# Attention, experts and second layer on one core: clears planned behind the scatters, one PSUM set, small DMAs moved off GpSimd's queue

## The chip, the cores and the metric

One core of a Trainium2 chip runs the whole program. The time is that of one execution on the device, in microseconds (us); the kernel before takes 758.77 us (median of 3 runs, 758.49 to 759.9). The engines are TensorE (PE; PEld is its weight load), VectorE (DVE), ScalarE (ACT), GpSimd (POOL) and SyncE (SP), which mainly issues DMAs.

## The reference, cut to what matters

Three layers follow each other: a linear attention with a decayed state, a top-1 mixture of 8 experts, and a dense two-matrix layer.

```python
for t in range(S):                                  # batch 4, heads 8, S 768, head_dim 48
    state = alpha[:, :, t, :, None] * state + np.einsum('bhd,bhe->bhde', k[:, :, t], v[:, :, t])
    y[:, :, t] = np.einsum('bhd,bhde->bhe', q[:, :, t], state)
x = y.transpose(0, 2, 1, 3).reshape(B * S, H * D)   # 3072 tokens of 384
expert_idx = np.argmax(normalised(x) @ normalised(expert_emb).T / tau, axis=1)
for e in range(8):
    mask = expert_idx == e
    h = np.maximum(x[mask] @ w1[e], 0.0)            # 384 -> 1024
    out[mask] = gate_w[mask, None] * (h @ w2[e])    # 1024 -> 384
h = out @ w_in                                      # 384 -> 2048
result = np.maximum(0.01 * h, h) @ w_out            # 2048 -> 384
```

## The kernel before, in words

**First stage, 0 to some 178 us.** Attention runs in 16 units (a batch and two heads each); its last matmuls of a unit are the values (L426, `py<-am,v`), whose sums ScalarE and VectorE copy to `yT` (L469, L471), and TensorE turns these back (L486) for the routing of a batch. The routed rows are written by 6 indirect DMAs of GpSimd for each batch (L609, 24 in all) to `bucket` in DRAM, where each expert owns a region; a row carries 384 values, its scale, its gate and its token's number. `early_rows` (L613 ff.) reads the first 256 rows of expert 0 back as soon as the third batch's scatters have landed, so that expert 0 can begin before the last batch is there. After the last batch VectorE works out at which place of the packed order each expert begins (`offi`, L760).

**Experts, some 178 to 391 us.** Each of 8 experts takes up to CAP = 432 rows. `gather` loads them from `bucket` (`xg`, L921, L924), `block` casts them to two f16 halves `xs` (L976), SP's DMA transposes turn them (`xt<-xs`, L978). `up` (L1036 to L1038) multiplies by w1 into 4 PSUM banks `ps1`; ScalarE and VectorE empty a bank together (`held<-ps`, L1043 and L1044). `down` (L1062 to L1064) multiplies by w2 into 4 banks `ps2`, emptied into the packed `x2h` and `x2l` (L1073, L1074) at a place that each engine loads from `offi` (L1050). Expert 0 goes in two parts, 256 early columns and the other 176. The weights come as pieces through four staging tiles: a DMA on SP (L987), then `w1h<-wstage` on ScalarE (L992) and `w1l<-wstage,w1h` on VectorE (L993). `clear` (L1083) fills the rest of `x2` by 12 ScalarE copies of 128x660. `put_meta` (L935 to L947) copies gate and token number of each expert's rows into the packed `meta` in DRAM: one DMA for expert 0 and two for each of the others, 15 in all, on GpSimd's queue. The chunks of 432 rows overlap (a later expert's rows overwrite the end of the chunk before), so each of these DMAs waits for the one before to have landed.

**Second layer, 391 to 752 us.** 12 groups of 256 columns run through `u` (5 banks, L823 to L825) and `c` (3 banks, L857 to L859); their PSUM pool is opened when that of the experts has been released. `ms` is loaded from `meta` (L1286) and its second column cast to the indices `tki` (L1299), which the output's indirect stores (L891) use.

**What sets the order.** Nothing is scheduled by hardware or compiler here. `Plan` (L31 ff.) takes each step with an engine, a cost, what it reads and writes and a wished time `at`, sets the steps out against each other as if each took its cost, and writes each engine's instructions in the order of the starts that come out of that. Engines then run strictly in this order, and wait by semaphores. A step of `clear` has no reads, so the planner may put it anywhere:

```python
plan.add(S_, 0.16 + w / 1200, lambda x=x: nc.scalar.activation(x, row0[:, 0:1].to_broadcast([P, w]), AF.Copy), [], [("clear", n, d)], at=at)
```

The steps of experts and second layer go through two separate plans, each in a `with tc.manual_schedule():` of its own.

Of the kernel before, what the change touches and what calls it, by code (L numbers as in the profile page):

```python
# [21 lines left out]
P = 128  # L22
# [3 lines left out]
D = H * HD  # L26
# [149 lines left out]
def body(ctx, tc, qT, kT, aT, v, emb, tau, w1, w2, w_in, w_out, out):  # L176
# [24 lines left out]
    nc.gpsimd.dma_start(tau_sb, tau.to_broadcast([P, 1]))  # L201
# [10 lines left out]
    hid = [[held[:, i, f] for f in range(NF1)] for i in range(2)]  # L212
    shared = keep.tile([P, 2 * W64], F32, name="shared")
# [67 lines left out]
    with tc.tile_pool(name="at", bufs=1) as rt, \  # L281
# [53 lines left out]
        nc.gpsimd.dma_start(emb_sb, emb)  # L335
# [83 lines left out]
        def values(i, h):  # L419
            b, hp = divmod(i, NP)  # L420

            def go():
                for n in range(HC):
                    for j in range(2):
                        c, e0 = HC * h + n, (2 * hp + j) * HD
                        nc.tensor.matmul(y_of(c, j), tv[b % 2][:, c, e0:e0 + HD], tam[h][:, j, n], start=c == 0, stop=c == NC - 1)  # L426

# [466 lines left out]
    first = [stage() for _ in range(4)]  # L894
    with tc.tile_pool(name="mx", bufs=1) as mxp, \
            tc.tile_pool(name="w64", bufs=1) as w64, \
            tc.tile_pool(name="wst2", bufs=1) as wst2, \
            tc.tile_pool(name="pm", bufs=1, space=PSUM) as pm:
# [7 lines left out]
        ps1 = [pm.tile([P, CAP], F32, name=f"ps1{i}") for i in range(4)]  # L906
        ps2 = [pm.tile([P, CAP], F32, name=f"ps2{i}") for i in range(4)]
# [27 lines left out]
        def put_meta(e):  # L935
            xg = xgs[e % 2]

            def go():
                if e == 0:
                    nc.gpsimd.dma_start(meta[:CAP], bucket[:CAP, D + 1:D + 3])  # L940
                    return
                so = nc.gpsimd.value_load(offi[0:1, e:e + 1], min_val=0, max_val=NT)
                nc.gpsimd.dma_start(meta[ds(so, NF * P)].rearrange("(n p) c -> p n c", p=P), xg[:, :NF, D + 1:D + 3])
                if CAP % P:
                    nc.gpsimd.dma_start(meta[ds(so + NF * P, CAP % P)], xg[:CAP % P, NF, D + 1:D + 3])

            plan.add(G_, 6.0, go, [("xg", e % 2)] if e else ["bucket"], [("meta", e)], at=begin(e) + 4)  # L947
# [137 lines left out]
        with tc.manual_schedule():  # L1085
            plan.add("WAIT", 10.8, lambda: None, [], ["bucket"])
# [304 lines left out]
```

## Time and profile before

| what | value |
|---|---|
| median of the runs | 758.77 us (758.49 to 759.9) |
| the profiled execution, its own time | 762.96 us |
| span of its trace | 761.3 us |
| mean granted clock of TensorE | 0.99 |
| PE busy | 729.9 us, 96% of the span, 6774 matmuls |
| DVE, ACT, POOL busy | 601.3, 388.4 and 99.8 us |
| DMA | 84.70 MB in 58769 packets, mean 111 GB/s |

TensorE is busy almost always, so the table says little. What a change can win or lose lies in the few stretches where TensorE stands, and the views that show these are the waits, the timeline by engine and the table by stretch. The profiled execution is 4.2 us slower than the median; differences are counted against its own time.

### The profile page before, as it was taken

What the parts mean: (1) busy time and instruction counts of PE and PEld (TensorE: products, weight loads), DVE (VectorE), ACT (ScalarE), POOL (GpSimd) and SP (SyncE); (2) the same over time, 40 slices, a digit from 0 to 9 for tenths busy, and PEclk for the clock granted to TensorE, in tenths of its full rate; (3) what the DMA queues carried; (4) which work ended last, traced back from release to release, by engine and by line L of the source; (5) the groups of instructions that cost most, each with busy time, mean ns of one, the idle gap of its engine ahead of it and who ended that gap; (6) DMA issues with size and microseconds to landing.
All of it is one profiled execution on the core that took longest, in us unless ns stands there. A gap on an engine that the chain in (4) does not pass through costs nothing.

```text
span 761.3 us, 16644 instructions
## 1 busy us (share of the span) xinstructions
PE 729.9 (96%) x6774; PEld 561.6 (74%) x6774; DVE 601.3 (79%) x1131; ACT 388.4 (51%) x746; POOL 99.8 (13%) x108
## 2 busy tenths in 40 slices
PE   7999999967999999999989999999999999999995
PEld 4777767745855555555558777999999999999994
DVE  8989899953887789888869888878768778778761
ACT  3344544535876668767736454544544444445430
POOL 6121715132000100000000011010010110110111
PEclk9999999998999999999999999999999999999998
DMA  8983946233999897886500000000000000000000
GB/s 287 357 284 128 284 147 197 75 112 112 235 244 258 174 239 203 228 231 205 171 1 2 12 11 11 13 22 2 22 22 2 22 22 1 22 22 2 22 23 24
DMA packets 58769, 84.70 MB, mean 111 GB/s; under 512 B 26680, under 2 KB 37952, under 8 KB 58688
## 3 DMA queue, kind: packets, MB, share of 16 engines
q1 hardware_dynamic: 55072, 74.06, 35.2%
q0 software_dynamic: 3616, 9.53, 3.4%
q8 instruction: 55, 0.90, 0.5%
q14 instruction: 26, 0.21, 0.1%
HBM read 66.80 MB, written 12.12 MB: 104 GB/s over the span
## 4 chain that ended last, share of the span: by engine, by line
PE 84%; DVE 7%; DMA 3%; ACT 2%; issue 1%; POOL 1%; another core or an unknown queue 1%; SPq 0%; ACTq 0%; POOLq 0%; DVEq 0%
PE u L823 8%; PE u L824 8%; PE u L825 8%; PE c L857 6%; PE c L859 6%; PE c L858 6%; PE ps L1036 4%; PE ps L1037 4%; PE ps L1038 4%; PE ps L1063 4%; PE ps L1064 4%; PE ps L1062 4%; PE psc L407 3%; DMA v<-in_v 2%; PE py L426 2%; PE py L458 2%
## 5 line engine op out<-in xcount | busy, mean ns | idle before, releaser
L823 PE MATMUL u<-x2h,wih 128*128 128x256 f16 x576 | 157.0, 273 | 2.1 <-DVE x2l L1074 2.1
L824 PE MATMUL u<-x2l,wih 128*128 128x256 f16 x576 | 157.0, 273 | 0.0
L825 PE MATMUL u<-x2h,wil 128*128 128x256 f16 x576 | 157.0, 273 | 0.0
L831 DVE TENSOR_TENSOR held<-u,held 128x512 f32<-128x512 f32 x96 | 65.9, 687 | 56.0 <-ACT held L830 55.9
L830 ACT ACTIVATE held<-u 128x512 f32<-128x512 f32 x96 | 57.3, 597 | 86.5 <-PE u L825 83.1
L891 POOL DMA_INDIRECT out<-wstage,tki x24 | 25.2, 1049 | 437.0 <-DVE wstage L870 257.1
L1063 PE MATMUL ps<-held,w2h 128*128 128x432 f16 (+2 forms) x216 | 70.2, 326 | 0.3 <-DVE held L1044 0.3
L1062 PE MATMUL ps<-held,w2h 128*128 128x432 f16 (+2 forms) x216 | 70.2, 326 | 0.0
L1064 PE MATMUL ps<-held,w2l 128*128 128x432 f16 (+2 forms) x216 | 70.2, 326 | 0.0
L1037 PE MATMUL ps<-xt,w1h 128*128 128x432 f16 (+1 forms) x192 | 63.6, 333 | 0.8 <-DVE xt L962 0.8
L1036 PE MATMUL ps<-xt,w1h 128*128 128x432 f16 (+1 forms) x192 | 63.6, 333 | 0.4 <-ACT xt L961 0.4
L1038 PE MATMUL ps<-xt,w1l 128*128 128x432 f16 (+1 forms) x192 | 63.6, 333 | 0.0
L824 PEld LDWEIGHTS <-wih 128*128 128x128 f16 x576 | 56.4, 98 | 9.1 <-issue 2.4
L823 PEld LDWEIGHTS <-wih 128*128 128x128 f16 x576 | 56.4, 98 | 6.8
L825 PEld LDWEIGHTS <-wil 128*128 128x128 f16 x576 | 56.4, 98 | 6.5
L1044 DVE SCALAR_TENSOR_TENSOR held<-ps,held 128x432 f16<-128x432 f32 (+2 forms) x72 | 39.1, 551 | 16.0 <-ACT held L1043 15.8
L1043 ACT ACTIVATE held<-ps 128x432 f16<-128x432 f32 (+2 forms) x72 | 34.9, 487 | 20.7 <-PE ps L1038 20.4
L870 DVE SCALAR_TENSOR_TENSOR wstage<-c,ms,wstage 128x192 f32<-128x192 f32 x80 | 31.8, 411 | 16.9 <-PE c L859 16.8
L347 PE MATMUL pfill<-busy,ones 128*128 128x512 f16 x121 | 39.9, 403 | 2.1 <-POOL busy L194 2.1
L1037 PEld LDWEIGHTS <-w1h 128*128 128x128 f16 x216 | 21.4, 99 | 20.7 <-issue 6.1
L842 ACT ACTIVATE o0h<-held 128x256 f16<-128x256 f32 (+1 forms) x40 | 20.9, 523 | 30.7 <-DVE held L831 30.0
L842 ACT ACTIVATE o1h<-held 128x256 f16<-128x256 f32 (+1 forms) x40 | 20.9, 523 | 30.7 <-DVE held L831 29.9
(272 smaller groups left out, 1918.1 us busy)
## 6 DMA issues: line engine op xcount, KB each, us to landing
wstage<-in_w SPq DMA_DIRECT2D x64, 384.0 KB, 4.5
a<-in_aT SPq DMA_DIRECT2D x16, 387.5 KB, 6.1
k<-in_kT SPq DMA_DIRECT2D x16, 384.0 KB, 10.6
q<-in_qT SPq DMA_DIRECT2D x16, 384.0 KB
wstage<-in_w_in SPq DMA_DIRECT2D x16, 384.0 KB, 5.8
wstage<-in_w_out SPq DMA_DIRECT2D x16, 384.0 KB, 3.0
v<-in_v SPq DMA_DIRECT2D x8, 576.0 KB, 6.2
xg<-bucket SPq DMA_DIRECT2D x6, 582.0 KB
```

What stands on the lines that cost most here:

```text
L823: nc.tensor.matmul(d, wih[:, k, fs], xs[0][k], start=k == 0, stop=False)
L824: nc.tensor.matmul(d, wih[:, k, fs], xs[1][k], start=False, stop=False)
L825: nc.tensor.matmul(d, wil[:, k, fs], xs[0][k], start=False, stop=k == KD - 1)
L830: add("ACT", 0.59, lambda: nc.scalar.activation(dst, src, AF.Copy, scale=0.01), [key], [("g", i)])
L831: add("DVE", 0.69, lambda: nc.vector.tensor_tensor(dst, src, dst, op=ALU.max), [key, ("g", i)], [("g", i)])
L857: nc.tensor.matmul(d, oh, wh, start=k == 0, stop=False)
L1036: nc.tensor.matmul(ps, w1h[:, f, k], xt[:, k], start=k == 0, stop=False)
L1037: nc.tensor.matmul(ps, w1h[:, f, k], xt[:, KD + k], start=False, stop=False)
L1038: nc.tensor.matmul(ps, w1l[:, f, k], xt[:, k], start=False, stop=k == KD - 1)
L1062: nc.tensor.matmul(ps, w2h[:, f, ds_], hh, start=f == 0, stop=False)
L1063: nc.tensor.matmul(ps, w2h[:, f, ds_], hl, start=False, stop=False)
L1064: nc.tensor.matmul(ps, w2l[:, f, ds_], hh, start=False, stop=f == NF1 - 1)
```

## The change

Five things are done.

- `tau` and `expert_emb` are loaded on ScalarE's DMA queue and not on GpSimd's.
- `put_meta` issues one DMA for each expert, from `bucket` to `meta`, both in DRAM, 432 rows of 8 bytes, on SP's queue; SP loads the place from `offi` first. These are 8 DMAs for 15. All write the one key "meta", and the loading of `ms` and the cast to `tki` move from the second layer's plan into that of the experts (`scales`).
- `clear` reads "bucket", which the planner holds to be there 10.8 us after its start; so it plans the clears behind the scatters.
- Experts and second layer share one set of 8 PSUM banks, which stays open over both, and one scheduled region: `banks` is `ps1` and the first of `ps2`, `sums` the other three of `ps2`.
- One matmul of ones (`pfill`) follows the last values of the attention.

```diff
-    nc.gpsimd.dma_start(tau_sb, tau.to_broadcast([P, 1]))
+    nc.scalar.dma_start(tau_sb, tau.to_broadcast([P, 1]))
...
-        nc.gpsimd.dma_start(emb_sb, emb)
+        nc.scalar.dma_start(emb_sb, emb)
...
+                if i == NU - 1 and h:
+                    keep_busy("f")
...
+    both = ExitStack()
+    pm = both.enter_context(tc.tile_pool(name="pm", bufs=1, space=PSUM))
...
-        ps1 = [pm.tile([P, CAP], F32, name=f"ps1{i}") for i in range(4)]
-        ps2 = [pm.tile([P, CAP], F32, name=f"ps2{i}") for i in range(4)]
+        ps1, ps2 = ([pm.tile([P, 2 * PAIR], F32, name=f"{n}{i}") for i in range(4)] for n in ("ps1", "ps2"))
...
         def put_meta(e):
-            xg = xgs[e % 2]
-
             def go():
-                if e == 0:
-                    nc.gpsimd.dma_start(meta[:CAP], bucket[:CAP, D + 1:D + 3])
-                    return
-                so = nc.gpsimd.value_load(offi[0:1, e:e + 1], min_val=0, max_val=NT)
-                nc.gpsimd.dma_start(meta[ds(so, NF * P)].rearrange("(n p) c -> p n c", p=P), xg[:, :NF, D + 1:D + 3])
-                if CAP % P:
-                    nc.gpsimd.dma_start(meta[ds(so + NF * P, CAP % P)], xg[:CAP % P, NF, D + 1:D + 3])
-
-            plan.add(G_, 6.0, go, [("xg", e % 2)] if e else ["bucket"], [("meta", e)], at=begin(e) + 4)
+                so = nc.sync.value_load(offi[0:1, e:e + 1], min_val=0, max_val=NT) if e else 0
+                nc.sync.dma_start(meta[ds(so, CAP) if e else slice(0, CAP)], bucket[e * NT:e * NT + CAP, D + 1:D + 3])
+
+            plan.add(Q_, 1.5, go, ["bucket"], ["meta"], at=begin(e) + 4, size=(CAP * 64, 5.0))
+
+        def scales():
+
+            plan.add(Q_, 0.5, lambda: nc.sync.dma_start(ms, meta[:NT].rearrange("(n p) c -> p n c", p=P)), ["meta"], ["ms"], size=(NT * 8, 4.0), at=begin(E - 1) + 6)
+            plan.add(V, 0.2, lambda: nc.vector.tensor_copy(tki, ms[:, :, 1]), ["ms"], ["tki"], at=begin(E - 1) + 12)
...
-                    plan.add(S_, 0.16 + w / 1200, lambda x=x: nc.scalar.activation(x, row0[:, 0:1].to_broadcast([P, w]), AF.Copy), [], [("clear", n, d)], at=at)
+                    plan.add(S_, 0.16 + w / 1200, lambda x=x: nc.scalar.activation(x, row0[:, 0:1].to_broadcast([P, w]), AF.Copy), ["bucket"], [("clear", n, d)], at=at)
...
-        banks = [pn.tile([P, 2 * PAIR], F32, name=f"u{i}") for i in range(5)]
-        sums = [pn.tile([P, 512], F32, name=f"c{i}") for i in range(3)]
+        banks, sums = ps1 + ps2[:1], ps2[1:]
```

**ScalarE at the start of the experts.** These are its rows from the second half of the early columns (`shared<-ptr`, L633, in the changed kernel L637) on; `row` to `x2h` or `x2l` is a clear, `held<-ps` the emptying of an early column bank. Before:

```order
L633 ACTIVATE shared<-ptr_172 128x3x128
L633 ACTIVATE shared<-ptr_173 128x3x128
L1083 ACTIVATE x2h_1870<-row_86 128x660
L1083 ACTIVATE x2l_1873<-row_86 128x660
L1043 ACTIVATE held<-ps_1911 128x256
L1083 ACTIVATE x2h_1870<-row_86 128x660
L1043 ACTIVATE held<-ps_1912 128x256
L1083 ACTIVATE x2l_1873<-row_86 128x660
L1043 ACTIVATE held<-ps_1913 128x256
L1050 TENSOR_LOAD offi
```

And with the change:

```order
L637 ACTIVATE shared<-ptr_174 128x3x128
L637 ACTIVATE shared<-ptr_175 128x3x128
L1052 TENSOR_LOAD offi
L1052 ISA x2
L1045 ACTIVATE held<-ps_1914 128x256
L1045 ACTIVATE held<-ps_1915 128x256
L1045 ACTIVATE held<-ps_1916 128x256
L1045 ACTIVATE held<-ps_1917 128x256
L1045 ACTIVATE held<-ps_1914 128x256
L1045 ACTIVATE held<-ps_1915 128x256
L994 ACTIVATE w1h<-wstage 128x768
```

The two clears ahead of the first `held` are gone, the load of expert 1's place from `offi` has come to the front, and six banks are emptied in a row.

**SP in expert 1.** `xg_1901` is the gather for expert 3, `xt_1902` what the transposes for expert 2 write, and `wstage` a weight piece. Before, from that gather to the last of these transposes:

```order
L924 DMA xg_1901<-bucket 128x3x388
L921 DMA xg_1901<-bucket 48x388
L987 DMA wstage<-in_w 128x768
L987 DMA wstage<-in_w_in 128x768
L987 DMA wstage<-in_w 128x768 x2
L978 DMA_TRANSPOSE xt_1902<-xs_1905 128x6x128
L978 DMA_TRANSPOSE xt_1902<-xs_1906 128x6x128
L987 DMA wstage<-in_w_in 128x768
L978 DMA_TRANSPOSE xt_1902<-xs_1907 128x6x128
L978 DMA_TRANSPOSE xt_1902<-xs_1908 128x6x48
```

And with the change, from the copy of expert 2 (L942 is `put_meta`, L948 `ms`) to the first transpose for expert 2 (now `xt_1905`); left out are the loadings of the places:

```order
L942 DMA meta<-bucket 432x2
L989 DMA wstage<-in_w 128x768
L989 DMA wstage<-in_w_in 128x768
...
L942 DMA meta<-bucket 432x2
L989 DMA wstage<-in_w 128x768
...
L942 DMA meta<-bucket 432x2
...
L942 DMA meta<-bucket 432x2
...
L942 DMA meta<-bucket 432x2
...
L942 DMA meta<-bucket 432x2
L948 DMA ms<-meta 128x24x2
L989 DMA wstage<-in_w 128x768
L980 DMA_TRANSPOSE xt_1905<-xs_1908 128x6x128
```

Ahead of the first row stand the same gather and one piece. The copies of experts 2 to 7 and `ms` stand one behind the other, each waiting on SP for the landing of the copy before, and the third piece of expert 2's w1 and all four transposes for expert 2 have come to stand behind them.

**PE at the end of the attention.** Before, the last values and what follows them:

```order
L347 MATMUL pfill<-busy,ones_75 128x512
L458 MATMUL py<-rc_124,st_136 48x128 x4
L426 MATMUL py<-am_130,v_121 48x128 x6
L486 MATMUL ptr_172<-ident,yT_140 128x112 x3
L486 MATMUL ptr_173<-ident,yT_140 128x112 x3
```

And with the change:

```order
L462 MATMUL py<-rc_126,st_138 48x128 x4
L428 MATMUL py<-am_132,v_123 48x128 x6
L349 LDWEIGHTS ones_75
L349 MATMUL pfill<-busy,ones_75 128x512
L490 MATMUL ptr_174<-ident,yT_142 128x112 x3
```

A weight load and a matmul that wait for nothing now stand between the last values and the turning of `yT`, which waits for ScalarE's copy of these values.

## Rows read from the trace of the kernel before

**Rows 1.** Waits of PE, 0 to 200 us: us, times, longest us.

```profile
PE ps L1036 <- DVE held L1044: 5.5, 1, 5.5
PE ptr L486 <- ACT yT L469: 3.7, 1, 3.7
```

**Rows 2.** Waits of PE, 200 to 400 us.

```profile
PE u L823 <- DVE x2l L1074: 2.1, 1, 2.1
```

**Rows 3.** Table by stretch: length, busy of PE, PEld, DVE, ACT, POOL, clock, DMA share.

```profile
160.00:162.00 2.00, 2.00 (x11) 0.56 (x14) 0.75 (x2) 0.86 (x2) 0.00 (x0) 0.50 0.69 199
236.00:262.00 26.00, 26.00 (x144) 13.96 (x143) 19.78 (x35) 16.93 (x32) 2.88 (x5) 1.00 0.94 241
420.00:540.00 120.00, 120.00 (x1106) 102.40 (x1104) 97.42 (x209) 56.17 (x91) 10.23 (x11) 1.00 0.04 14
```

**Rows 4.** Timeline of ACT, 176 to 180 us: start, us, instruction, wait before it.

```profile
177.53 0.75 ACT L1083 ACTIVATE x2h<-row 128x660 f32<-128x660 f32 x1 [8.87 <-DMA bucket<-xb,slot]
...
178.83 0.36 ACT L1043 ACTIVATE held<-ps 128x256 f16<-128x256 f32 x1
```

**Rows 5.** Timeline of DVE, 171 to 180 us.

```profile
171.37 0.27 DVE L760 CAST offi<-ohs 128x8 int32<-128x8 f32 x1
```

**Rows 6.** Timeline of PE, early columns of expert 0.

```profile
170.11 0.27 PE L1036 MATMUL ps<-shared,w1h 128*128 128x256 f16 x1 [0.41 <-DVE ohs L757]
...
173.92 0.27 PE L1038 MATMUL ps<-shared,w1l 128*128 128x256 f16 x1
179.70 0.37 PE L1036 MATMUL ps<-shared,w1h 128*128 128x256 f16 x1 [5.51 <-DVE held L1044]
...
183.44 0.27 PE L1036 MATMUL ps<-shared,w1h 128*128 128x256 f16 x1
...
193.26 0.80 PE L956 MATMUL ps<-ident,xs 128*128 128x128 f32 x6
```

**Rows 7.** Timeline of PE, first matmul of expert 1 and last of expert 7.

```profile
206.81 0.35 PE L1036 MATMUL ps<-xt,w1h 128*128 128x432 f16 x1
...
390.59 0.35 PE L1064 MATMUL ps<-held,w2l 128*128 128x432 f16 x1
```

**Rows 8.** Timeline of PE and ACT, end of the attention.

```profile
154.55 0.86 PE L426 MATMUL py<-am,v 128*48 128x128 f32 x12
...
158.61 0.71 ACT L469 ACTIVATE yT<-py 112x384 f32<-112x384 f32 x2 [5.09 <-remote]
```

**Rows 9.** Timeline of SP, 176 to 220 us.

```profile
186.06 0.33 SPq L987 DMA_DIRECT2D wstage<-in_w  x1
...
196.01 5.27 SPq L978 DMA_TRANSPOSE xt<-xs  x4
206.21 0.44 SPq L987 DMA_DIRECT2D wstage<-in_w  x1
...
210.44 2.63 SPq L978 DMA_TRANSPOSE xt<-xs  x2
```

**Rows 10.** DMA issues, 176 to 240 us: KB each, median us from issue to landing.

```profile
xg<-bucket SPq DMA_DIRECT2D x4, 194.0 KB, 5.3
...
xt<-xs SPq DMA_TRANSPOSE x12, 4.6
```

**Rows 11.** Timeline of SP and DVE around the border of the experts and second layer.

```profile
390.97 0.38 SPq L1286 DMA_DIRECT2D ms<-meta  x1
...
394.44 0.18 DVE L1299 CAST tki<-ms 128x24 uint32<-128x24 f32 x1 [1.42 <-DMA ms<-meta]
```

**Rows 12.** Table by stretch, 392 to 394 us: its 8-byte transfers alone.

```profile
392.00:393.00 1.00, 0.00 (x0) 0.00 (x0) 1.00 (x2) 0.00 (x0) 0.00 (x0) 1.00 0.85 13
393.00:394.00 1.00, 0.93 (x9) 0.83 (x9) 0.02 (x1) 0.00 (x0) 0.00 (x0) 1.00 0.83 12
```

**Rows 13.** Waits of POOL, whole span, and the first of them in its timeline.

```profile
POOL meta L945 <- DMA meta<-xg: 37.3, 6, 8.6
...
199.77 0.54 POOL L945 DMA_DIRECT2D meta<-xg  x1 [4.30 <-DMA meta<-xg]
```

More of the change, by code (lines that the diff above doesn't have):

```diff
@@ L212, in body @@
     hid = [[held[:, i, f] for f in range(NF1)] for i in range(2)]
+    ms = keep.tile([P, TT, 2], F32, name="ms")
+    tki = keep.tile([P, TT], U32, name="tki")
     shared = keep.tile([P, 2 * W64], F32, name="shared")
@@ L894, in body @@
     first = [stage() for _ in range(4)]
+    both = ExitStack()
+    pm = both.enter_context(tc.tile_pool(name="pm", bufs=1, space=PSUM))
     with tc.tile_pool(name="mx", bufs=1) as mxp, \
             tc.tile_pool(name="w64", bufs=1) as w64, \
-            tc.tile_pool(name="wst2", bufs=1) as wst2, \
-            tc.tile_pool(name="pm", bufs=1, space=PSUM) as pm:
+            tc.tile_pool(name="wst2", bufs=1) as wst2:
         sets = [w_first, expert_tiles(mxp)]
@@ L1132, in body @@
-    with tc.tile_pool(name="gp", bufs=1) as gp, \
-            tc.tile_pool(name="pn", bufs=1, space=PSUM) as pn:
-        ms = gp.tile([P, TT, 2], F32, name="ms")
-        tki = gp.tile([P, TT], U32, name="tki")
+                    plan.add(S_, 0.16 + w / 1200, lambda x=x: nc.scalar.activation(x, row0[:, 0:1].to_broadcast([P, w]), AF.Copy), ["bucket"], [("clear", n, d)], at=at)
+        both.enter_context(tc.manual_schedule())
+        plan.add("WAIT", 10.8, lambda: None, [], ["bucket"])
+        second = second_pieces()
@@ new lines, in body, with pieces_of, add @@
+        per = -(-len(second) // E)
+        def pieces_of(e):
+            mine = [(begin(e) + 4.0 + 2.9 * j, weights, e + 1, j) for j in range(2 * KD * F1 // CH if e + 1 < E else 0)]
+            mine += [(begin(e) + 5.0 + 5.8 * j, *second[e * per + j]) for j in range(min(per, len(second) - e * per))]
+            return sorted(mine, key=lambda x: x[0])
+        def add(mine):
+            for at, go, *args in mine:
+                go(*args, at)
+        for f in range(NF1):
+            up(0, f, xte, f - 40.0, slice(0, E0), True)
@@ new lines, in body @@
+        for d in range(KD):
+            down(0, d, d - 30.0, slice(0, E0), True)
+        mine = pieces_of(0)
+        add(mine[:6])
+        gather(0)
+        gather(1)
+        add(mine[6:])
+        for n in range(E0 // P, NB):
+            first_rows(n)
+        for e in range(E):
+            if e:
+                add(pieces_of(e))
+            cols = slice(0 if e else E0, CAP)
+            for f in range(NF1):
+                up(e, f, xts[e % 2][:, :, cols], begin(e) + 1.65 * f - 12.0, cols)
+                if e + 1 < E and f < NB:
+                    block(e + 1, f)
+                if f == 2:
+                    put_meta(e)
+                if f == 4 and e + 2 < E:
+                    gather(e + 2)
+            if e:
+                places(e)
+            for d in range(KD):
+                down(e, d, begin(e) + 13.2 + 4.4 * d - 12.0, cols)
+            if e == 0:
+                for d in range(KD):
+                    clear(d, begin(1) + 4.0 * d)
@@ L1136, in body @@
+        scales()
+        for i in plan.order():
+            plan.ops[i][2]()
+    with tc.tile_pool(name="gp", bufs=1) as gp:
         oviews = dram_disjoint_views(out, TT)
-        banks = [pn.tile([P, 2 * PAIR], F32, name=f"u{i}") for i in range(5)]
-        sums = [pn.tile([P, 512], F32, name=f"c{i}") for i in range(3)]
+        banks, sums = ps1 + ps2[:1], ps2[1:]
         flat = held.rearrange("p i f t -> p (i f t)").bitcast(F32)
```

83 lines of the change are left out of this document (20 added, 63 removed).

## The prediction, made before the changed kernel was run

> **What bounds the kernel now.** The waits of TensorE come first, because TensorE is busy for 96% of the span. Up to 200 us there are two long ones [rows 1]: 5.5 us for the emptying of a bank of expert 0, and 3.7 us at the turn of the attention's last `yT`; after 200 us there is one, 2.1 us at the border of the second layer [rows 2]. The table by stretch shows that the rest is full: 26.00 busy of 26.00 us in an expert, 120.00 of 120.00 in the second layer [rows 3]. So the change can win these 11 us and what the clock loses behind them, and no more; it can lose without limit wherever it makes TensorE wait in a stretch that is full now. The timelines show why it stands, and what SP does meanwhile.
>
> **Clears behind the scatters.** ScalarE waits 8.87 us for the last scatters at the first clear, and the first emptying of a bank, which needs only the early columns, stands behind that clear until 178.83 [rows 4]. TensorE filled its four banks from 170.11 to 173.92 and then stood for 5.51 us [rows 6]. In the new order the load of a place and then six emptyings stand there. That load needs `offi`, ready at 171.64 [rows 5]; so the first emptying can begin around 172.2, before the fourth bank is full, and the 5.5 us go. The clock goes with them: 18 matmuls from 179.70 to 183.44 take 3.74 us, at 0.109 us each, as between 170.11 and 173.92, they would take 1.96 [rows 6]; 1.8 us more. After that the part runs on to 193.26 without another long wait, when the rest of expert 0 begins [rows 6]. This needs `xg`, whose gather stands on SP behind a weight piece at 186.06 [rows 9] that waits for ScalarE's and VectorE's casts of the piece before. These stand behind the same emptyings and move with them, so I take the whole of it: **-7.2 us** (sum of 5.5 and 1.8, less 0.1 for the start). The clears themselves (12 of 0.75 us, 9 us of ScalarE) now lie later on ScalarE, which is busy 16.93 of 26.00 us in an expert [rows 3]; expert 1's first `x2` needs its own clears only, so I cost them at nothing. Without that cover the bound is the 2 us of three clears in a row.
>
> **One PSUM set.** TensorE stands 2.1 us at the border since the second layer's pool opens only when the experts' last bank is empty [rows 2]. The first five of its steps use 30 matmuls on two thirds of `x2`, which were there before, so with shared banks they run meanwhile: **-2.1 us**. The bounds are 0 and -2.1.
>
> **The matmul behind the last values.** These end by the trace at 155.41 (154.55 and 0.86), ScalarE's copy of them starts at 158.61 with nothing before it but a wait [rows 8]. Over 3 us lie between, and the only thing peculiar to the place is that what follows them on TensorE waits for that very copy. If the release of the banks is held up until TensorE has something else to run, the added matmul takes it away, and everything up to the last scatter moves: between 0 and 3.2 us, and with the clock at 0.50 behind the gap [rows 3] some 1 us more. I take **-3.1 us**, as the row at the place itself says, without the clock. The Trainium skill's page "Perfetto Trace Analysis" (section "Tensor Engine Instruction (MATMUL, LD_WEIGHTS)") says that the end of a matmul in a profile is an estimate and no observation; by it the copy may have followed the true end, and the term would be 0, the first rival below.
>
> **Small DMAs.** `tau` and `emb` are issued at the start, where loads wait for data anyhow; 0 us, with 0.5 us either way if ScalarE's first step is late. On GpSimd, 15 copies go; nobody on TensorE waits for GpSimd then, so this gives 0 in itself. On SP it costs, and this is the term that decides. Copies 2 to 7 and `ms` are seven issues with six landings waited for between, and behind them stand expert 2's third w1 piece and its four transposes. The piece at 206.21 [rows 9] marks the place of copy 2 in the old order; with the 7.2 us it is at 199.0. A landing costs, by the rows: for `ms` on empty queues 3.5 us from 390.97 to 394.44 [rows 11], of which 1.7 is the moving of 3072 small pieces (0.85 and 0.83 of two us) [rows 12], so some 2.4 us with the issue for 432 pieces; for GpSimd's copies beside other loads 4.3 us at the least and 6.2 on average (37.3 by 6) [rows 13]. Copies 2, 3 and 4 have weight pieces or `xg` right ahead of them on the queue: I take the shortest loaded one and 0.1 us of issue, 4.4 us each. Copies 5, 6 and 7 have nothing ahead, since SP itself waits: 2.4 us each. That is 20.4 us, and `ms` is issued at 219.4. After it come the piece and the transposes with four other issues: four transposes at 1.3 us each (5.27 for 4) [rows 9] and six issues of 0.4 make 7.6 us; the last transpose is issued 1.3 us before that and lands 4.6 us after [rows 10]. So expert 2's columns are there at 230.3. TensorE wants them at its next expert: one takes 26.3 us (206.81 to 390.9, by 7) [rows 7], and expert 1 now begins at 199.6, so at 225.9. It stands for 4.4 us. In the old order the transposes were begun at 210.44 [rows 9] with the same demand at 233.1, so nothing stood. Behind such a wait the clock falls as it did after 5.51 us: 1.8 us more [rows 6]. **+6.2 us.** The later experts don't repeat it, as no copies are left; SP, which was waiting for free stages before, catches up. Without a stall the bound is 0; if each landing takes 6.2 us, the chain takes 37.2, the columns come at 247.1, and the term is 21.2 and 1.8, +23.
>
> **Sum.** -7.2 - 2.1 - 3.1 + 6.2 = -6.2 us against the profiled execution's 762.96: 756.8. This stands 4.2 us above the median of the runs, so I expect a median of **752.6 us**.
>
> **Rivals.** *The last values gain nothing.* For it: the waits show no second place of this kind [rows 1, 2], so a rule of the engine is made of one case. Against: nothing else that the copy needs ends within these 3.2 us [rows 8]. The rest stays, -3.1 us: 755.7.
>
> *The chain is hidden.* If a landing costs 2.4 us even with loads ahead, six take 14.4, `ms` goes out at 213.4, the columns land at 224.3, before 225.9; the stall and its clock are gone: -12.4, 746.4. For it: a copy is 3.4 KB, and SP stops feeding the queue while it waits. Against: GpSimd's copies in that stretch never landed within 4.3 us [rows 13], and the DMA share was 0.94 in 236 to 262 [rows 3]. The skill's page "DMA: Bandwidth & Descriptors" (section "Anatomy of one DMA") puts about 2.0 us fixed on a DMA whatever its size, most of it the receipt of the write; by that figure six landings are an estimated 12 us and this rival is the case. The `ms` row agrees, the rows of GpSimd's copies do not.
>
> *The chain is longer than the gains.* One mechanism: SP, first in line for all loads, stands for each landing while expert 2's transposes are queued behind it. It decides from the mean landing at which the stall eats the other three terms, 12.4 less 1.8 of clock = 10.6 us: columns at 236.5, `ms` at 225.6, 26.6 us for six, **4.4 us each** where I have 3.4. With 5.0 us each `ms` goes at 229.0, the columns come at 239.9, the stall is 14.0 and the sum -12.4 + 14.0 + 1.8 = +3.4: 762.2. With 6.2 it is +10.6: 769.4. For it: these are GpSimd's own numbers [rows 13], and both ends of the new copies lie in DRAM. Against: GpSimd's copies ran beside SP's loads, and these run while SP issues none.
>
> *The change doesn't do what it says at the border.* Were the first steps of the second layer still held by a bank, 2.1 us of the sum would be missing; the order shows them free, and this lies within the range.
>
> **How the numbers follow.** A measurement of this kernel tells 0.2%, 1.5 us, from no change. The forecast has a chance of 0.33, the last values without gain 0.20, the hidden chain 0.22, the long chain 0.25. The forecast is faster by far unless its stall is 5 us longer (0.30 of 0.33); the first rival lies 1.6 us inside the faster side, and half a landing more takes it out (0.12 of 0.20); the hidden chain is faster in nearly all (0.21); the long chain hardly ever (0.03). That makes 0.66 faster. Slower are 0.19 of the long chain, 0.02 of the first rival and 0.01 of the forecast, 0.22 together; 0.12 are left for the same. The range goes from the hidden chain with the gap's clock counted in, 746, to a long chain of some 5.5 us a landing, 765; beyond that lies the rest of the long chain, about 0.1, and some 0.08 below.
>
> **What would show it.** In the profile of the changed kernel TensorE's wait of 5.5 us for `held` is gone and its matmuls follow at 0.109 us through the early columns; the wait at `u` is gone; ScalarE's copy of the last `yT` starts within 1 us of the last values, or after 3 us again. SP's timeline shows the copies to `meta`: their distance is the landing, 2.4, 3.4 or above 4.4 us. TensorE then waits 4 to 5 us for the `xt` of expert 2, at its first `ps` after expert 1, with the clock at half behind it. The forecast is wrong if that wait is absent or above 10 us, or if ScalarE, with the clears moved among expert 1's steps, holds up banks.

## The result and the profile after

The changed kernel takes 768.5 us (median; 768.36 to 769.51) where the kernel before takes 758.7 in the same comparison: ratio **1.0129, interval 1.0111 to 1.0146**, 9.8 us slower. The forecast was 752.6 us with a range up to 765. What happened is the mechanism of the third rival, SP standing for its own copies. That the time also comes near the 769.4 us which it gives for 6.2 us a landing is luck: the landings were shorter than that, and other terms failed with them.

TensorE's waits after 200 us in the profile after (us, times, longest us); those of before are [rows 2]:

```profile
PE ps L1038 <- DMA xt<-xs: 14.8, 1, 14.8
```

The 2.1 us at the border are gone, and 14.8 us at the first matmul of expert 2 have come, above the 10 us that were to show the forecast wrong. Up to 200 us the wait for `held` (5.5 us, [rows 1]) is gone and so is that for the last `yT` (3.7 us). The largest there are now these:

```profile
PE ptr L396 <- DVE kh L384: 3.3, 4, 1.7
PE pfill L349 <- POOL busy L194: 2.0, 1, 2.0
```

SP's timeline after shows why expert 2 is late (start, us, instruction; the old order is in [rows 9]):

```profile
200.22 0.58 SPq L942 DMA_DIRECT2D meta<-bucket  x1
201.29 0.34 SPq L989 DMA_DIRECT2D wstage<-in_w  x1
201.75 0.36 SPq L989 DMA_DIRECT2D wstage<-in_w_in  x1
206.60 0.60 SPq L942 DMA_DIRECT2D meta<-bucket  x1
207.30 0.55 SPq L989 DMA_DIRECT2D wstage<-in_w  x1
211.19 11.26 SPq L942 DMA_DIRECT2D meta<-bucket  x4
225.74 0.40 SPq L948 DMA_DIRECT2D ms<-meta  x1
226.25 1.65 SPq L989 DMA_DIRECT2D wstage<-in_w  x1
227.95 2.62 SPq L980 DMA_TRANSPOSE xt<-xs  x2
230.62 0.57 SPq L989 DMA_DIRECT2D wstage<-in_w_in  x1
231.29 1.22 SPq L980 DMA_TRANSPOSE xt<-xs  x1
232.56 1.04 SPq L989 DMA_DIRECT2D wstage<-in_w  x2
233.70 0.38 SPq L989 DMA_DIRECT2D wstage<-in_w_in  x1
234.17 1.99 SPq L980 DMA_TRANSPOSE xt<-xs  x1
```

From the copy of expert 2 at 200.22 SP issues nine DMAs ahead of `ms` at 225.74, six copies and three weight pieces, in 25.5 us; the last four landings take (225.74 - 211.19) / 4 = 3.64 us each, with next to nothing else under way (DMA share 0.00 to 0.12 from 214 to 226 us). Only then come the weight piece and the transposes.

Why the plan put the copies side by side stands in `Plan.order`: a step waits for `end[d]` of a step on another engine, but only for `start[d] + ops[d][1]`, its issue, of one on its own. The copies carry a landing of 5.0 us in the plan, but as each waits for another on SP, the next could be planned 1.5 us behind it.

The piece is missing on ScalarE too, which keeps its order and waits 16.41 us for it (timeline of ACT):

```profile
213.16 0.84 ACT L994 ACTIVATE w1h<-wstage 128x768 f16<-128x768 f32 x1 [0.48 <-DMA wstage<-in_w]
231.24 0.84 ACT L994 ACTIVATE w1h<-wstage 128x768 f16<-128x768 f32 x1 [16.41 <-DMA wstage<-in_w]
```

The casts of expert 2's own rows are not behind that piece. The last of them is this one on VectorE, nine us before `ms` is issued; what stands behind the piece are the casts for expert 3:

```profile
215.89 0.60 DVE L978 SCALAR_TENSOR_TENSOR xs<-xg,xs 48x384 f16<-48x384 f32 x1
```

TensorE's timeline has the start of expert 1, the end of its last matmul, expert 2, the end of expert 7 and the first matmul of the second layer; before, [rows 7] answer to the first and the fourth:

```profile
199.95 0.35 PE L1038 MATMUL ps<-xt,w1h 128*128 128x432 f16 x1
...
226.05 0.35 PE L1066 MATMUL ps<-held,w2l 128*128 128x432 f16 x1
241.18 0.52 PE L1038 MATMUL ps<-xt,w1h 128*128 128x432 f16 x1 [14.78 <-DMA xt<-xs]
...
269.09 0.35 PE L1038 MATMUL ps<-xt,w1h 128*128 128x432 f16 x1
```

Expert 2 takes 269.09 - 241.18 = 27.9 us where the others take 26.3: the clock behind the wait costs 1.6 us. The table by stretch shows the clock fall while TensorE stands and rise again some way into expert 2 (columns as in [rows 3]; the clock is the third figure from the right):

```profile
220.00:230.00 10.00, 6.39 (x36) 3.23 (x33) 0.00 (x0) 0.00 (x0) 0.00 (x0) 1.00 0.33 29
230.00:240.00 10.00, 0.00 (x0) 0.00 (x0) 7.16 (x13) 6.38 (x12) 0.00 (x0) 0.54 1.08 242
240.00:250.00 10.00, 8.82 (x40) 4.40 (x41) 7.46 (x13) 6.91 (x13) 0.00 (x0) 0.77 1.06 333
```

Expert 1 itself began 6.9 us earlier than before (199.95 against 206.81, [rows 7]), although the attention ended later. Taken apart by stretch, the two profiled executions differ so:

| stretch | before, us | after, us | difference | forecast |
|---|---|---|---|---|
| start to the last values | 154.55 | 157.21 | +2.7 | 0 |
| last values to first early column | 15.56 | 11.38 | -4.2 | -3.1 |
| first early column to expert 1 | 36.70 | 31.36 | -5.3 | -7.2 |
| expert 1 to the last matmul of expert 7 | 183.78 | 200.36 | +16.6 | +6.2 |
| border | 2.48 | 0.18 | -2.3 | -2.1 |
| second layer and end | 368.2 | 366.3 | -1.9 | 0 |

These sum up to +5.6, and the two executions stand 768.53 to 762.96. The medians stand 9.8 apart, because the profiled execution of before was 4.2 us above its own median. The second row says what was special about it: the copy of the last values came 3.2 us late there, and at once in the changed kernel's profile. The experiments show that this is no gain of the change. The 1.9 us in the second layer no run explains.

### The profile page after: what moved, and what is told of

It is laid out like the page before. It is cut to its first block, busy times and chain, and to the rows that moved or that the text cites. A ratio compares the mean times of both kernels' runs of the same rounds, so it can differ in the third digit from the quotient of the medians.

```text
span 766.8 us, 16571 instructions
## 1 busy us (share of the span) xinstructions
PE 730.8 (95%) x6775; PEld 561.6 (73%) x6775; DVE 602.4 (79%) x1131; ACT 389.0 (51%) x746; POOL 87.6 (11%) x91
## 3 DMA queue, kind: packets, MB, share of 16 engines
q0 software_dynamic: 3072, 9.49, 3.3%
## 4 chain that ended last, share of the span: by engine, by line
PE 81%; DMA 7%; DVE 7%; ACT 3%; issue 1%; POOL 0%; SPq 0%; POOLq 0%; DVEq 0%; ACTq 0%
PE ps L829 8%; PE ps L828 8%; PE ps L827 8%; PE ps L861 6%; PE ps L863 6%; PE ps L862 6%; PE ps L1038 4%; PE ps L1039 4%; PE ps L1040 4%; PE ps L1066 4%; PE ps L1065 4%; PE ps L1064 4%; DMA meta<-bucket 3%; PE psc L409 2%; PE py L462 2%; DMA wstage<-in_w 2%
## 5 line engine op out<-in xcount | busy, mean ns | idle before, releaser
L827 PE MATMUL ps<-x2h,wih 128*128 128x256 f16 x576 | 157.0, 273 | 0.0
L828 PE MATMUL ps<-x2l,wih 128*128 128x256 f16 x576 | 157.0, 273 | 0.0
L829 PE MATMUL ps<-x2h,wil 128*128 128x256 f16 x576 | 157.0, 273 | 0.0
L835 DVE TENSOR_TENSOR held<-ps,held 128x512 f32<-128x512 f32 x96 | 65.8, 686 | 51.3 <-ACT held L834 51.3
L834 ACT ACTIVATE held<-ps 128x512 f32<-128x512 f32 x96 | 57.2, 596 | 78.1 <-PE ps L829 77.9
L1038 PE MATMUL ps<-xt,w1h 128*128 128x432 f16 (+1 forms) x192 | 64.3, 336 | 15.7 <-DMA xt<-xs 14.8
L874 DVE SCALAR_TENSOR_TENSOR wstage<-ps,ms,wstage 128x192 f32<-128x192 f32 x80 | 31.9, 411 | 16.6 <-PE ps L863 16.5
## 6 DMA issues: line engine op xcount, KB each, us to landing
a<-in_aT SPq DMA_DIRECT2D x16, 387.5 KB, 5.4
```

What stands on the lines that cost most here:

```text
L827: nc.tensor.matmul(d, wih[:, k, fs], xs[0][k], start=k == 0, stop=False)
L828: nc.tensor.matmul(d, wih[:, k, fs], xs[1][k], start=False, stop=False)
L829: nc.tensor.matmul(d, wil[:, k, fs], xs[0][k], start=False, stop=k == KD - 1)
L834: add("ACT", 0.59, lambda: nc.scalar.activation(dst, src, AF.Copy, scale=0.01), [key], [("g", i)])
L835: add("DVE", 0.69, lambda: nc.vector.tensor_tensor(dst, src, dst, op=ALU.max), [key, ("g", i)], [("g", i)])
L1038: nc.tensor.matmul(ps, w1h[:, f, k], xt[:, k], start=k == 0, stop=False)
```

## The experiments

The kernel before takes 758.8 us on some chips and 763.7 to 764.8 on others. All experiments are therefore given as ratios to it on the same chip.

| run | what it is | ratio to the kernel before (95% interval) |
|---|---|---|
| the change | | 1.0129 (1.0111 to 1.0146) |
| e13_changed_again | the change once more, another chip | 1.0117 (1.0095 to 1.0139) |
| e1_spread | copies planned with their experts | 0.9904 (0.9878 to 0.993) |
| e2_pool | copies on GpSimd, `ms` late | 0.9913 (0.9886 to 0.9941) |
| e3_small_back | tau, expert_emb back on GpSimd | 1.0113 (1.0081 to 1.0146) |
| e4_spread_small | e1 and e3 | 0.9876 (0.9854 to 0.9897) |
| e6_clears_free | e4, clears unplanned again | 0.9945 (0.9926 to 0.9963) |
| e7_fill_alone | before, one matmul more | 0.9996 (0.9981 to 1.0012) |
| e9_small_alone | before, tau, expert_emb on ScalarE | 1.0013 (1.0 to 1.0027) |
| e10_clears_alone | before, clears behind the scatters | 0.9958 (0.9939 to 0.9977) |
| e11_fill12 | e4, twelve matmuls behind the last values | **0.9841** (0.9819 to 0.9864) |

e8_rows48 and e12_tau_moved were executed once each, under the profiler, and have no ratio. In e8_rows48 rows of `meta` are left out, so what it stores is not the result.

### Who stands while the copies land

e1_spread:

```diff
-            plan.add(Q_, 1.5, go, ["bucket"], ["meta"], at=begin(e) + 4, size=(CAP * 64, 5.0))
+            plan.add(Q_, 1.5, go, [("xg", e % 2)] if e else ["bucket"], ["meta"], at=begin(e) + 4, size=(CAP * 64, 5.0))
```

> The changed kernel with one edit: each copy to `meta` is planned with its expert's rows (as before the change) and no longer as soon as SP is free; the copies stay on SP, one for each expert, each still waiting for the one before, but in different experts. Theory A (SP standing for six landings with expert 2's transposes behind it cost the time): the 14.8 us wait for `xt` and the 1.6 us of clock behind it go, 768.5 - 16.4 = 752 us, 751 to 754. Rival B (the loads of expert 2 are late for another reason, such as ScalarE's order or the queue's load): a wait of 5 us or more for `xt` stays at expert 2, 757 us or above.

The copies now stand between 188 and 266 us on SP, and what is left of TensorE's waits after 200 us is this:

```profile
PE ps L1065 <- DVE held L1046: 0.5, 1, 0.5
```

The ratio falls from 1.0129 to 0.9904, by 17 us of 764; 14.8 and 1.6 were expected to go. Theory A holds. By this run alone a doubt is left, since the planner also set steps of ScalarE and VectorE in another order when the copies moved; e2_pool answers it.

e2_pool keeps the copies in one chain as in the change, but on another queue:

```diff
-                so = nc.sync.value_load(offi[0:1, e:e + 1], min_val=0, max_val=NT) if e else 0
-                nc.sync.dma_start(meta[ds(so, CAP) if e else slice(0, CAP)], bucket[e * NT:e * NT + CAP, D + 1:D + 3])
+                so = nc.gpsimd.value_load(offi[0:1, e:e + 1], min_val=0, max_val=NT) if e else 0
+                nc.gpsimd.dma_start(meta[ds(so, CAP) if e else slice(0, CAP)], bucket[e * NT:e * NT + CAP, D + 1:D + 3])
...
-            plan.add(Q_, 1.5, go, ["bucket"], ["meta"], at=begin(e) + 4, size=(CAP * 64, 5.0))
+            plan.add(G_, 1.5, go, ["bucket"], ["meta"], at=begin(e) + 4, size=(CAP * 64, 5.0))
...
-            plan.add(Q_, 0.5, lambda: nc.sync.dma_start(ms, meta[:NT].rearrange("(n p) c -> p n c", p=P)), ["meta"], ["ms"], size=(NT * 8, 4.0), at=begin(E - 1) + 6)
+            plan.add(Q_, 0.5, lambda: nc.sync.dma_start(ms, meta[:NT].rearrange("(n p) c -> p n c", p=P)), ["meta", ("xg", 1)], ["ms"], size=(NT * 8, 4.0), at=begin(E - 1) + 6)
```

> The changed kernel with its eight copies issued by GpSimd, as early and as close as before, each still waiting for the one before; only the loading of `ms` stands later on SP, behind the last gather, so that SP waits for none of them. tau and expert_emb stay on ScalarE's queue. Theory A (what costs is who stands while the copies land): the chain is as long on GpSimd, 3 to 5 us from copy to copy, and TensorE has no wait for `xt` at expert 2; the time is that of e1_spread, 0.988 to 0.993 of the kernel before. Rival B (the copies disturb the loads, whoever issues them): a wait of 3 us or more for `xt` at expert 2, 0.997 or above.

Its timeline of POOL, with the wait before each copy and what ended it:

```profile
196.44 0.61 POOL L942 DMA_DIRECT2D meta<-bucket  x1 [4.57 <-DMA meta<-bucket]
200.66 0.61 POOL L942 DMA_DIRECT2D meta<-bucket  x1 [3.60 <-DMA meta<-bucket]
208.78 0.61 POOL L942 DMA_DIRECT2D meta<-bucket  x1 [7.51 <-DMA meta<-bucket]
217.29 0.61 POOL L942 DMA_DIRECT2D meta<-bucket  x1 [7.90 <-DMA meta<-bucket]
224.32 0.61 POOL L942 DMA_DIRECT2D meta<-bucket  x1 [6.41 <-DMA meta<-bucket]
```

From one copy to the next it is 4.2, 8.1, 8.5 and 7.0 us here, beside SP's loads, mostly longer than on SP and beyond the 3 to 5 us expected. Yet TensorE has no wait after 200 us at all, and the ratio is that of e1_spread. So no cost of the copies themselves is seen: the cost was that the queue which loads everything else stood for them.

### What a landing is made of

```diff
-                nc.sync.dma_start(meta[ds(so, CAP) if e else slice(0, CAP)], bucket[e * NT:e * NT + CAP, D + 1:D + 3])
+                nc.sync.dma_start(meta[ds(so, 48) if e else slice(0, CAP)], bucket[e * NT:e * NT + (48 if e else CAP), D + 1:D + 3])
```

> The changed kernel with the copies of experts 1 to 7 cut from 432 rows of 8 bytes to 48; the rows left out of `meta` are simply missing, nothing else changes. It measures what a landing on SP is made of, at copies 5 to 7, which in the changed kernel are 3.64 us apart with nothing else on the queue. Theory A (it is a fixed time from issue to landing): 3.4 to 3.7 us apart, and TensorE's wait for `xt` falls by less than 2 us. Rival B (the small pieces set it, as I had it when I took 1.7 us off the `ms` row for its 3072 pieces): 2.6 us or less apart, and the wait falls by 4 us or more.

SP's timeline in this run:

```profile
211.64 10.29 SPq L942 DMA_DIRECT2D meta<-bucket  x4
224.31 0.40 SPq L948 DMA_DIRECT2D ms<-meta  x1
```

The last four landings take (224.31 - 211.64) / 4 = 3.17 us each, for a ninth of the rows; 432 rows took 3.64. So 0.47 us go with 384 small pieces, and by a straight line through the two some 3.1 us (an estimate) would be left for a copy of no rows at all. That is a little below what theory A named, and above rival B.

On TensorE's wait theory A missed: it is 10.6 us here, 4.2 less than in the change's profile, where less than 2 was named and rival B had 4 or more. The chain explains the fall. It begins at 202.87 and takes 21.4 us in place of 25.5: 1.9 us less in the last four landings, and 2.2 less in the two beside loads (4.58 and 4.19 us for 6.38 and 4.59). How much of the latter is the rows is open, since with 432 rows these two took 5.38 and 5.02 in e13_changed_again, where the wait was 13.9 us.

### The small loads at the start

The first change moved tau and expert_emb to ScalarE's queue. In the profile after, tau's load is issued at 0.82 us, beside that of `a` at 0.80; VectorE's first scan of the attention starts 2 us later than before, and waits for this load of `a` (timeline of DVE, after):

```profile
6.33 1.77 DVE L378 TENSOR_TENSOR_SCAN bc<-a,onesP 128x775 f32<-128x775 f32 x1 [3.01 <-DMA a<-in_aT]
```

And before:

```profile
4.25 1.77 DVE L376 TENSOR_TENSOR_SCAN bc<-a,onesP 128x775 f32<-128x775 f32 x1
```

e3_small_back puts both back:

```diff
-    nc.scalar.dma_start(tau_sb, tau.to_broadcast([P, 1]))
+    nc.gpsimd.dma_start(tau_sb, tau.to_broadcast([P, 1]))
...
-        nc.scalar.dma_start(emb_sb, emb)
+        nc.gpsimd.dma_start(emb_sb, emb)
```

> The changed kernel with one edit: the loads of tau and expert_emb go back to GpSimd's queue. Theory A (issued on ScalarE at 0.8 us, ahead of everything, their 160 small pieces slow the first load of `a`, on which VectorE starts at 6.33 us where it was 4.25): VectorE's first scan starts near 4.2 us again and the attention ends some 2 us earlier; but the chain of copies on SP starts with the scatters and moves along, so the time is 766 to 767 us. Rival B (a different spread of the loads in that one profile): first scan at 6 us or no change in time, 768.5 us.

The first scan starts at 4.15 us again. The wait at expert 2 is 13.2 us, and the ratio, 1.0113, can't be told from the change's. What the start gives is not seen behind the chain.

e4_spread_small has both edits:

> Both edits: copies planned with their experts, tau and expert_emb on GpSimd's queue. What is left of the change are the clears behind the scatters, the shared PSUM set, the matmul behind the last values and fewer copies. Theory A: 752 less 2 = 750 us, 748 to 751, that is some 9 us below the kernel before (7.2 for the clears, 2.1 for the border). If the matmul behind the last values is worth 3 to 4 us in runs without a profile too, 745 to 747. Rival B: a wait of TensorE in expert 1 or 2 stays and it is no better than 753 us.

Its median is 755.0 us, on a chip where the kernel before takes 763.65: 9.5 us are won in ratio (0.9876). From e1_spread to e4_spread_small the two small loads give 0.0028, 2.1 us, with intervals that overlap. e9_small_alone, the kernel before with the reverse of e3's edit, asks the same from the other side:

> The kernel before with tau and expert_emb loaded on ScalarE's queue, nothing else. Theory A (their small pieces go ahead of the first load of `a`, and VectorE's first scan starts 2 us later, which the whole attention follows): first scan at 6.2 to 6.4 us, ratio to the kernel before 1.001 to 1.003. Rival B (the late first scan is made good later, since other loads bound the first units anyhow): first scan late, ratio within 0.001 of 1.

The first scan starts at 6.49 us and the ratio is 1.0013 (1.0 to 1.0027): by the median about 1 us of the 2.2 us comes through to the end, and none at the edge of the interval, so theory A and rival B are not told apart. e12_tau_moved is e1_spread with one line back:

```diff
-        nc.scalar.dma_start(emb_sb, emb)
+        nc.gpsimd.dma_start(emb_sb, emb)
```

> e1_spread with expert_emb back on GpSimd's queue, so that of the two small loads tau alone (one value to 128 partitions) is on ScalarE's. It tells which of the two makes VectorE's first scan late. If tau: first scan at 5.5 us or later. If expert_emb (8 rows in 32 pieces): first scan before 4.6 us. Both a little: between.

With tau alone on ScalarE the first scan starts at 6.15 us. So tau, one value spread over 128 partitions, is enough for nearly all of the delay (expert_emb alone was not tried); the table of DMA queues of this run, 0 to 9 us, has its queue as 144 packets with no megabytes to speak of (packets, MB, share of 16 engines):

```profile
q1 hardware_dynamic: 789, 2.00, 64.5%
q10 hardware_dynamic: 144, 0.00, 0.8%
```

Why so small a share holds up the large load is open.

### The clears

e10_clears_alone is the kernel before with the one edit:

```diff
-                    plan.add(S_, 0.16 + w / 1200, lambda x=x: nc.scalar.activation(x, row0[:, 0:1].to_broadcast([P, w]), AF.Copy), [], [("clear", n, d)], at=at)
+                    plan.add(S_, 0.16 + w / 1200, lambda x=x: nc.scalar.activation(x, row0[:, 0:1].to_broadcast([P, w]), AF.Copy), ["bucket"], [("clear", n, d)], at=at)
```

> The kernel before with one edit: the clears read `bucket` and are planned behind the scatters. Theory A: TensorE's wait of 5.5 us for `held` is gone, expert 1 begins 7 us earlier, the border's wait of 2.1 us stays; 7.2 us of 764 are won, ratio 0.989 to 0.992. Rival B (what is won is given back, because the copies of GpSimd or the gather then come too late for expert 1): a wait of 3 us or more for `xt` at expert 1 or 2, ratio 0.995 or above.

The wait for `held` falls from 5.5 to 0.8 us, the border's stays (2.7 us), no wait for `xt` comes; so TensorE's waits are as theory A has them. But the ratio is 0.9958, 3.2 us (1.8 to 4.7 by the interval), which is rival B's, without the wait that should have caused it. Its table by stretch has a clock of 0.50 where the kernel before had 0.88 in its own profile:

```profile
160.00:172.00 12.00, 11.96 (x57) 6.67 (x56) 5.31 (x28) 3.74 (x9) 1.33 (x2) 0.50 0.13 38
```

The edit need not be the cause. e9_small_alone, on the same chip and with the clears where they stood before, has the same in this stretch:

```profile
160.00:172.00 12.00, 10.96 (x52) 6.08 (x53) 5.56 (x28) 3.96 (x10) 0.00 (x0) 0.52 0.14 44
```

e6_clears_free takes the clears out of e4_spread_small by the reverse of the same edit:

> e4_spread_small with the clears again without a read, so that the planner puts them ahead of the first emptying as before the change. Theory A (the clears behind the scatters are worth the 5.5 us wait and 1.8 us of clock): the wait of TensorE for `held` is back with 5 to 6 us, and the ratio to the kernel before rises from 0.9876 by 7 us of 764, to 0.996 to 0.998. Rival B (the rest of expert 0 is bound by its gather in any case): it rises by less than 3 us, 0.991 or below.

The ratio goes from 0.9876 to 0.9945: 5.3 us of 764, between what theory A and rival B named. The wait is back with 3.9 us, less than the 5 to 6 expected:

```profile
183.85 0.27 PE L1038 MATMUL ps<-shared,w1h 128*128 128x256 f16 x1 [3.94 <-DVE held L1046]
```

So the clears are worth 3 to 5 us on these chips. e10_clears_alone rules out 7.2 there; e4 against e6 doesn't by itself, since both intervals are some 0.002 wide to either side.

A reason that four profiles agree with, though no run sets out to test it: where the clock is at half ahead of the early columns, they begin later, the scatters land meanwhile, and less is left to wait for. With the clears ahead, the wait is 5.5 us in the kernel before and e7_fill_alone (clock 0.88 and 0.86 in 160 to 172 us), and 3.9 in e6_clears_free and e9_small_alone (0.54 and 0.52), whose early columns begin at 175.83 and 175.52 instead of 170.11 [rows 6]. From 3.9 us to e10's 0.8 there are 3.1 to be won, about what e10 measures.

### The late release of the last values

e7_fill_alone is the kernel before with the change's added matmul:

```diff
+                if i == NU - 1 and h:
+                    keep_busy("f")
```

> The kernel before with the one matmul of ones behind the last values of the attention, nothing else. Theory A (the release of the last values waits until TensorE has something to run): ScalarE's copy starts at once in the profile and the timed runs win 3 to 4 us, 754.5 to 755.5. Rival B (the late release belongs to the profiled execution, which is 4.2 us above its kernel's median; 3.2 us of release and 1.1 of clock are 4.3): the profile shows the copy at once, and the timed runs stay at 758.7, within 0.5 us.

The ratio is 0.9996. And the release is not even on time in its profile. ScalarE's copy of the last values, whose matmuls end at 157.55 by the trace, starts here:

```profile
160.91 0.71 ACT L471 ACTIVATE yT<-py 112x384 f32<-112x384 f32 x2 [5.25 <-remote]
```

In the changed kernel's own profile it had started at once (the matmuls end at 158.07):

```profile
158.12 0.71 ACT L473 ACTIVATE yT<-py 112x384 f32<-112x384 f32 x2 [1.93 <-PE py L428]
```

So the added matmul gains nothing in time, and doesn't bring the release on time either; rival B named the time rightly and the profile wrongly. The release was 3.1 to 3.4 us late in the profiles of all experiments from e1 to e12, with or without the matmul. What goes with it beyond these 3 us is the clock: TensorE stands, and from 160 to 172 us the clock is 0.50 to 0.54 in seven of these profiles (e10_clears_alone among them) and 0.86 in three; in the changed kernel's own, with the release on time, it is 0.89. e11_fill12 puts work there:

```diff
                 if i == NU - 1 and h:
-                    keep_busy("f")
+                    for _ in range(12):
+                        keep_busy("f")
```

> e4_spread_small with twelve matmuls of ones behind the last values in place of one, 2.6 us at full clock. In most profiles taken so far the release of the last values is 3.2 us late, whether one matmul follows or none, and TensorE's clock is at half for 4 to 12 us behind. Theory A (the release is late for a cause that TensorE's own work does not touch, and the half clock is the price of standing): the release stays 3 us late where it is late, the clock stays at 1.00 through it, and the median falls by 1 to 4 us against e4_spread_small, ratio 0.983 to 0.986. Rival B (the release needs more work behind it than one matmul): the release is on time as well, ratio 0.982 or below. Rival C (the matmuls stand in the way where the release is on time): no gain, 0.987 or above.

The release is late all the same (matmuls end at 159.28, copy at 162.46), and the clock stays at full in this stretch (in the next 12 us it is 0.86, where e4 had 0.93):

```profile
160.00:172.00 12.00, 9.34 (x68) 4.93 (x66) 6.10 (x30) 4.72 (x12) 1.98 (x3) 1.00 0.21 69
```

The ratio is 0.9841 against e4's 0.9876. The intervals (0.9819 to 0.9864, 0.9854 to 0.9897) overlap by a little, so the 2.7 us are likely rather than shown, and the clock is that of one execution. This is the fastest version of the study: 752.6 us where the kernel before takes 764.8.

Last, the changed kernel again, on another chip:

> The changed kernel once more, unedited, on the chip of the other experiments. In its own profile the last values were released at once, in all experiments 3.2 us late. Theory A (the late release comes and goes by execution and has nothing to do with the added matmul): the release is 3 us late here too, the wait for `xt` at expert 2 is 12 to 15 us as before, and the ratio is 1.008 to 1.015. Rival B (the unedited kernel releases at once, so one of my edits brought the delay back): release within 0.3 us.

The release is on time here (copy at 157.11, matmuls end at 157.06), the wait at expert 2 is 13.9 us, and the ratio 1.0117. Theory A's late release did not come. Of the 14 profiles just two have the release on time, and both are of the unedited changed kernel, so rival B isn't dismissed. Against it, the late release was there in the kernel before's own profile [rows 8], which has none of my edits, and in this comparison the kernel before took 758.8 us, as beside the change, where it had taken 763.7 to 764.8 beside the late ones. I take it to go with the chip or the execution, which is not shown: no edited kernel was profiled on a chip of the faster kind. What causes it stays open.

## Why the prediction was wrong

**The step that failed is the stall of TensorE at expert 2, which I put at 4.4 us: the price of a landing on SP in it, and the way from the chain to expert 2's columns.** Measured were 14.8 us. For the six landings I took three loaded ones at 4.4 us and three empty ones at 2.4, 20.4 us in all; it was 25.5. Two were loaded, 6.38 (206.60 - 200.22) and 4.59 (211.19 - 206.60), and the other four took 3.64 each.

The 4.4 came from a wait and not from a landing. The 4.30 us of [rows 13] are the time that GpSimd stood after it had issued the copy before, and this issue takes time as well:

```profile
194.64 0.82 POOL L943 DMA_DIRECT2D meta<-xg  x1 [16.22 <-ACT xt L961]
```

From there to the next copy at 199.77 it is 5.13 us.

The 2.4 came from the `ms` row, 3.5 us from issue to the cast [rows 11], less 1.7 us for the moving of its 3072 pieces [rows 12], with something added for 432 pieces and the issue. But `ms` is a load into SBUF, and the copies end in DRAM. Loads into SBUF that move 384 KB each landed in 3.0 us in the kernel before (DMA issues, whole span: KB each, median us from issue to landing):

```profile
wstage<-in_w_out SPq DMA_DIRECT2D x16, 384.0 KB, 3.0
```

The copies of e8_rows48 took longer than that, 3.17 us, for 48 rows of 8 bytes. So a price read from a load into SBUF did not hold for a copy inside DRAM. Whether the subtraction was wrong for `ms` too no run tells, as e8 changed the rows and not the destination. The Trainium skill's figure of about 2.0 us (page "DMA: Bandwidth & Descriptors", section "Anatomy of one DMA", where it is fitted to DMAs issued by GpSimd), by which the chain would have been hidden, is not what these DRAM-to-DRAM copies on SP show: 3.17 us at the least.

**What follows the chain was also too short.** From `ms` to expert 2's columns I had 10.9 us; it took 241.18 - 225.74 = 15.4. The five weight pieces and four transposes were counted rightly. But the last transpose is issued 8.4 us after `ms` (at 234.17), where I had 6.3, and its data are there 7.0 us later, where I had 4.6 [rows 10]. SP issued without a pause meanwhile and waited for no cast, and ScalarE's 16.41 us of waiting, which held up expert 3's casts, left no wait of TensorE behind. All that the chain had held up was now issued in one go, at a DMA share of 1.08 in 230 to 240 us; that this made the last landing longer is likely and was not tried. With the copy of expert 2 1.2 us later than I had it, 5.1 from the landings and 4.5 from here, and TensorE ready 0.5 us later, the stall is 14.8 instead of 4.4 us; its clock cost 1.6 against 1.8.

**The rival had the mechanism, and its time by luck.** It decided from a mean landing of 4.4 us; the mean was 25.5 / 6 = 4.25, below that. By its own sum 4.25 gives a stall of 9.5 us and 757.7 us in all, still faster than before. What carried the kernel beyond that is the 4.5 us behind the chain and the terms below. My argument against it, that SP issues no loads meanwhile, was true of the last four landings only; they were shorter for it (3.64 against 6.38 and 4.59), but not as short as 2.4.

**Clears.** The wait went as forecast, and with it the sign; the size was 5.3 us in the change's own profile, and 3 to 5 by e10 and e6. In that profile the 5.5 us of the wait are won and the 1.8 us of clock are not: the clock falls in the early columns there too, without the wait (table by stretch of the changed kernel, columns as in [rows 3]):

```profile
168.00:172.00 4.00, 3.57 (x21) 2.62 (x21) 2.02 (x12) 0.53 (x2) 3.08 (x4) 0.68 0.42 156
172.00:176.00 4.00, 4.00 (x35) 3.41 (x33) 1.49 (x4) 1.39 (x4) 1.63 (x2) 0.89 0.38 142
```

**Border.** Right: 2.48 us became 0.18 in the profile. No run has the shared set alone.

**The matmul behind the last values.** Wrong: 0 in time (e7_fill_alone). I read a mechanism out of a gap in one execution which I had already noted to be 4.2 us above its median. The gap of 3.2 us and the half clock behind it are about those 4.2 us, so the sum took them off twice, once as a gain of the change and once on the way to the median.

**Small loads at the start.** I costed them at 0 with 0.5 either way, because loads wait for data there anyhow. But the scan waits for the first load of `a`, and tau's load ran beside it: 2.1 us at the first scan, about 1 us at the end by e9's median.

The forecast was -6.2 us and +9.8 were measured. By the table of stretches, with its second row taken as nothing because it holds the 4.2 us by which one execution stood above the median, these 16.0 us are 10.4 of the stall and its clock, 3.1 of the last values, 2.7 at the start and 1.9 of the clears, less 1.9 in the second layer and 0.2 at the border.

## What to carry to other kernels

A chain of dependent DMAs belongs on a queue on which nothing else waits, or spread so far that each has landed before the next is due; on the queue that feeds the kernel, every landing is a stop for everything behind it. A planner that counts a landing only for steps of other engines won't see this: it put seven DMAs side by side because each cost it no more than its issue. The landing of a tiny DMA is best priced by a whole row of a tiny DMA between the same memories, and from one issue to the next; a wait alone leaves the issue out. And where the profiled execution is off its median, no term should rest on a gap that may be the reason.

## What was not expected of the hardware

- Copies between two places in DRAM took 3.17 us to land with 48 rows of 8 bytes and 3.64 with 432, on a queue with nothing else; beside loads it was 4.2 to 8.5 us from one copy of 432 rows to the next (e2_pool has both ends).
- One load of a single value to 128 partitions, issued at the same time as a 387.5 KB load on another queue, delayed the scan that waits for the latter by 2 us (6.15 against 4.15 us).
- The release of a finished group of matmuls came 3.2 us late in some executions and at once in others, with TensorE at work behind it or not. With TensorE idle for part of that time the granted clock was 0.50 over the 12 us from 160 to 172 us in several profiles, which is the lower of the two levels, 1.2 GHz; with twelve matmuls of ones it stayed at 1.00, 2.4 GHz.
